# Retention followed by a gated FFN: the 64x64 matmuls of a block in stretches of three, three and two items instead of four pairs

## The chip, the cores and the metric

One NeuronCore of a Trainium2 chip runs the whole program in one launch. The metric is the device time in microseconds (us) of one execution; the time before is the median of three runs, 890.47 us (888.77 to 890.8). The engines are called as in the profile: PE is TensorE's matmuls and PEld its weight loads, DVE is VectorE, ACT is ScalarE, POOL is GpSimd, SP is the engine that issues most DMAs.

## The reference, cut to what matters

```python
# q, k, v: (8 batches, 8 heads, 576 positions, 64)
scores = q @ k^T / 8                          # per batch and head
ret    = (scores * gamma[h] ** (i - j) where i >= j, else 0) @ v
x      = ret, laid out as (8 * 576 tokens, 512)
h      = x @ w_in                             # 512 -> 2048
out    = (h - tanh(h)) @ w_out                # 2048 -> 512
```

The retention can be computed position block by position block. With a block of 64 positions, the output of a block is q times a running state (the sum of k^T v over all earlier blocks) plus the block's own masked scores times v. The powers of gamma are put into q and v by tables, so that one 0/1 mask serves every block.

## The kernel before

**Blocks and items.** The 576 positions are nine blocks of 64 (numbered 0 to 8, `n` for the FFN, `c0` for the retention). A block has eight items, one per batch (`b`); item number `j` is 8 times the block plus `b`. The eight heads of an item lie as two halves of 64 partitions times four. The FFN of a block takes all 8 x 64 = 512 tokens at once.

**The two kinds of PE work.** The FFN is made of `mm1(n, f)` (L320, twelve 128x512 matmuls in words of fp32r: hidden slice `f` of 16) and `mm2(n, f)` (L379, twelve more, accumulated over all `f` in the four banks `o0` to `o3`). `activate` (L345) turns the result of `mm1` into the words `gh` and `gl`: tanh on ACT (L353), a subtraction on DVE (L354), a cast on ACT (L355), a subtraction on DVE (L356). The retention is made of 64x64 fp32 matmuls, all issued in `run` (L247, line L252 in the profile): `m_score` (8 calls per item), `m_state` (8), `m_out` (16). A call appears as two matmuls in the profile. `run` takes two lists and issues two calls of the one and two of the other in turn; scores and states use the two array quadrants on the diagonal, outputs use the other two, so that the two lists run side by side.

**An entry.** `entry(p, sc)` (L289) does, in one stretch of PE work, for the pair of items `2p`, `2p+1`: their outputs and state updates, and the scores of the next pair. Then DVE masks those scores into `pm` (L263, needed by the outputs of the next entry), ACT casts the outputs to `xh` (L278), DVE makes `xl` (L280) and adds the new state (L311). After that the next-but-one pair is loaded (1 MB, L171, on SP's queue) and scaled on POOL (`prep`, L185 and L186). `pm`, `new` and `own` have one buffer each, the PSUM tag `h` has two banks, which `mm1` and the scores `sc` share.

**The order of the work** is written out by hand, and `in_order` (L47) keeps every engine's instructions in the order in which they are written. The parts around the change are:

- L529 to L568 (`seq`): `mm1` of blocks 0 and 1, whose results are spilled, while the weights are converted to words by `step()` (a third of a weight tile per call: DVE L105, L110, L112, L124 and ACT L95, L98, L117); the entries of block 1 lie in it.
- L570 to L583 (`late`, 32 steps `k`): each step issues the two words of step `k+1` (`words`, ACT L375, DVE L376), the tanh and the subtraction of step `k+2` (`resume`, ACT L368, DVE L369), fetches a spilled tile, calls `step()` (twice while `k < 4`), and then issues `mm2`. Entries of block 2 stand ahead of `mm2` at `k` = 3, 8, 13 and 18.
- L585 to L596: for blocks `n` = 2 to 8, `mm1(n, f)` and the `mm2` of one slice earlier in turn; the four entries of block `n+1` stand between them at `f` = 1, 5, 9 and 13.

Of the kernel before, what the change touches and what calls it, by code (L numbers as in the profile page):

```python
# [9 lines left out]
F32 = mybir.dt.float32  # L10
# [9 lines left out]
P = 128  # L20
NF = DF // P
# [9 lines left out]
STEP = float(np.arctanh(0.5) / (1.06 * 2.0**-15))  # L31
WARM = 26

NP = NC * B // 2


class Parts:
# [30 lines left out]
def retention_ffn(ctx: ExitStack, tc: tile.TileContext, ins, out, spill):  # L68
# [81 lines left out]
            step()  # L150


    loaded, scored, xs, qtabs = {}, {}, {}, {}

    def load_qtab(c):
        if c not in qtabs:
# [6 lines left out]
    def load_pair(p, u=None):  # L163

        if p >= NP:
            return
        c, pr = divmod(p, B // 2)
        load_qtab(c)
        a = loaded["pair", p] if u == 1 else pool.tile([P, 2, 4, 4, C], F32, tag="a", name=f"a{p}")
        if u is None:  # L170
            nc.sync.dma_start(a, qkv_d[c - 1, 2 * pr : 2 * pr + 2].rearrange("u p t i s -> p u t i s"))  # L171
        else:
            nc.sync.dma_start(a[:, u], qkv_d[c - 1, 2 * pr + u])
        loaded[2 * p], loaded[2 * p + 1] = a[:, 0], a[:, 1]
        loaded["pair", p] = a
        loaded["qv", p] = a[:, :, 0], a[:, :, 2]

    def prep(p, q=True):
        if p >= NP:
            return  # L180
        c = p // (B // 2)
        a = loaded["pair", p]
        if q:
            table = qtabs[c].unsqueeze(1).broadcast_to([P, 2, 4, C])
            nc.gpsimd.tensor_tensor(a[:, :, 0], a[:, :, 0], table, op=ALU.mult)  # L185
        nc.gpsimd.tensor_tensor(  # L186
            a[:, :, 2], a[:, :, 2], vtab[:, c].unsqueeze(1).unsqueeze(3).broadcast_to([P, 2, 4, D]), op=ALU.mult
        )

    def load_early(p):
        c, pr = divmod(p, B // 2)
        if pr < 2:
            return load_pair(p)
        src = qkv_d[c - 1, 2 * pr : 2 * pr + 2].rearrange("u p t i s -> p u t i s")
        parts = []
        for t in range(2):
            parts.append(const.tile([P, 2, 2, 4, C], F32, tag=f"wo{2 * (pr - 2) + t}", name=f"a_early{p}_{t}"))
            nc.sync.dma_start(parts[t], src[:, :, 2 * t : 2 * t + 2])  # L200
            behind(tc, pace[-1])
        for u in range(2):
            loaded[2 * p + u] = Parts([part[:, u] for part in parts])
        loaded["qv", p] = parts[0][:, :, 0], parts[1][:, :, 0]

    def scale_q(p):
        q, table = loaded["qv", p][0], qtabs[p // (B // 2)]
        nc.vector.tensor_tensor(q, q, table.unsqueeze(1).broadcast_to([P, 2, 4, C]), op=ALU.mult)

    def scale_v(p):  # L210
        v = loaded["qv", p][1]
# [43 lines left out]
    def after_score(j, sc, n):  # L255

        if j < B:

            pm = pool.tile([P, 2, 4, C], F32, tag="gh", name=f"pm{j}")
            nc.vector.tensor_tensor(pm[:, 0], sc[:, 0], decay, op=ALU.mult)  # L260
        else:
            pm = pool.tile([P, 2, 4, C], F32, tag="pm", bufs=1, name=f"pm{j}")
            nc.vector.tensor_tensor(  # L263
                pm[:, :n].rearrange("p u i q -> p (u i) q"), sc.rearrange("p u i q -> p (u i) q"),
                mask.unsqueeze(1).broadcast_to([P, 4 * n, C]), op=ALU.mult,
            )
        for u in range(n):
            scored[j + u] = pm[:, u]
# [20 lines left out]
    def entry(p, sc, more=None):  # L289
        c0, pr = divmod(p, B // 2)  # L290
        new = psp.tile([P, 2, 4, D], F32, tag="new", bufs=1, name=f"new{p}")
        o = psp.tile([P, 2, 4, C], F32, tag="own", bufs=1, name=f"own{p}")
        same, other = [], []
        for u in range(2):
            if p + 1 < NP:
                same += m_score(2 * p + 2 + u, sc[:, u])
            other += m_out(2 * p + u, o[:, u])
        if c0 < NC - 1:
            for u in range(2):
                same += m_state(2 * p + u, new[:, u])  # L300
        if more is not None:
            same += more[0]
        run(same, other)
        if p + 1 < NP:
            after_score(2 * p + 2, sc, 2)
        after_out(2 * p, o, 2)
        if more is not None:
            more[1]()
        if c0 < NC - 1:
            st = state[:, 2 * pr : 2 * pr + 2]  # L310
            nc.vector.tensor_tensor(st, new, st, op=ALU.add)  # L311
        if p >= B:
            load_pair(p + 2)
            prep(p + 2)


    gs, ops, homes, obs = {}, {}, {}, {}
# [27 lines left out]
    def activate(n, f, h, g):  # L345
        if n == NC - 1 and f == NF - 1:

            both = pool.tile([P, 2, BLK], F32R, tag="a", name="both")
# [6 lines left out]
        nc.scalar.copy(gh, g)  # L355
        nc.vector.tensor_tensor(gl, g, gh.bitcast(F32), op=ALU.subtract)  # L356
        gs[n, f] = (gh, gl)
# [127 lines left out]
    for j in range(B):  # L485
        o = psp.tile([P, 8, C], F32, tag=("o2", "o3", "own")[j % 3], bufs=1, name=f"own_first{j}")[:, :4]
        run(score_first(j + 2) if j < B - 2 else [], m_out(j, o))
        if j < B - 2:
            after_score(j + 2, firsts[j + 2].unsqueeze(1), 1)
            paced(lambda: load_paced(7) if j == 0 else upto("load", j + 2) if j < 4 else None)  # L490
        if j == 3:
            nc.sync.dma_start(vtab, vtab_d)
            nc.sync.dma_start(krows[0], krows_d[0])
            load_early(B // 2)
            nc.sync.dma_start(mask, mask_d)
            upto("load", 7)
            load_early(B // 2 + 1)
        if j < 4:
            busy(*((2, BLK) if j < 2 else (1, BLK // 2)))
        low = after_out(j, o.unsqueeze(1), 1, j < 6)  # L500
        if j == 0:
            paced(lambda: upto("load", 2))
        if j >= 6:
            lows.append(low)
        if j < 4:
            step()
        if j == 5:
            guard(*stream[1], True)
        if j == 6:
            upto("guard", 2)  # L510
# [15 lines left out]
    late = [(1, f) for f in turn] + [(0, f) for f in range(NF)]  # L526
    early = {5: 4, 8: 5, 10: 6, 14: 7}
    scales = {2: 4, 4: 5, 7: 6, 9: 7, 13: 8}
    for k, (n, f) in enumerate(seq):  # L529
        last_two = k - (len(seq) - 2)  # L530
        if k in (2, 7):
            scale_k(k // 4)
        if k + 1 in early:
            scale_v(early[k + 1])
        if last_two < 0:
            step()
        else:
# [4 lines left out]
            if k < 24:  # L542
                step()
        if k in scales:
            scale_q(scales[k])
        upto("load", k + (7 if k < 11 else 6))
        if k in (2, 5):
            load_early(B // 2 + 2 + (k - 2) // 3)
        if k in (9, 10):
            load_pair(B, k - 9)  # L550
        for f in [f for f in home if home[f] == (7, 13, 12, 11, 10)[k - NF]] if NF <= k < NF + 5 else []:
            nc.sync.dma_start(spill[0, f], homes[home[f]][:, (f + 1) % 2 if f > 1 else f])
        if k == 3:
            nc.sync.dma_start(krows[1], krows_d[1])
            behind(tc, pace[-1])
            sc = scores_of(B // 2 - 1)
            ms, done = first_states(0, "new")
            run(m_score(B, sc[:, 0]) + m_score(B + 1, sc[:, 1]) + ms, [])
            after_score(B, sc, 2)
            done()  # L560
        if k in early:
            p = early[k]
            more = first_states(2 * (p - 3), f"o{(p + 1) % 2}") if p < B - 1 else None
            entry(p, scores_of(p), more)
        if k == 14:
            load_pair(B + 1)
        if k in (26, 28):
            prep(B + (k - 26) // 2, k == 28)  # L568
    p = B
    for k, (n, f) in enumerate(late):  # L570
        if 0 < k < len(late) - 1:
            words(*late[k + 1])
# [3 lines left out]
            fetch(*late[k + 4])  # L576
        for _ in range(2 if k < 4 else 1):
            step()
        if k in (3, 8, 13, 18):
            entry(p, psp.tile([P, 2, 4, C], F32, tag="h", bufs=2, name=f"s{n}_{f}"))  # L580
            p += 1
        if k < len(late) - 1:
            mm2(n, f)  # L583

# [69 lines left out]
```

## Time and profile before

| | |
|---|---|
| median of the runs | 890.47 us (888.77, 890.47, 890.8) |
| profiled execution | 891.8 us |
| span in it, first to last instruction | 890.0 us |
| PE matmuls, busy | 877.6 us |
| DVE, ACT, POOL busy | 363.3, 287.7, 67.7 us |
| mean granted TensorE clock | 0.995 |
| 64x64 stretches for blocks 2 to 8 | 28 |

Busy time of PE is the union of its matmuls from start to modelled end; matmuls overlap, so PE reads as busy even where a handover between two kinds of matmul costs time. Such costs are read from the start times of consecutive matmuls. A row of a timeline merges instructions of the same kind that follow each other; its first number is the start, its second the length of the merged piece.

### The profile page before, as it was taken

The page shows a single profiled execution, that of the slowest core. Times are in us where ns is not written, and L with a number is a line of the kernel's source. Part 1 is how long each engine was busy: PE and PEld are TensorE (multiplying, and loading weights), DVE is VectorE, ACT ScalarE, POOL GpSimd, SP SyncE. Part 2 cuts the span into 40 slices and gives each one's busy share as a digit, 9 for nine tenths or more (in the row PEclk, how much of TensorE's full clock was granted, in tenths as well). Part 3 has the DMA queues.
Part 4 walks back from the last instruction along what each step waited for, and adds up shares of the span by engine and source line. Part 5 has one row for each costly group of instructions (what it writes and reads, how often), then busy time and mean ns, then how long its engine had stood idle before and what let it go on. Part 6 is the DMA issues. An engine that isn't in the chain of part 4 may idle for free.

```text
span 890.0 us, 17595 instructions
## 1 busy us (share of the span) xinstructions
PE 877.6 (99%) x7848; PEld 724.3 (81%) x7848; DVE 363.3 (41%) x548; ACT 287.7 (32%) x503; POOL 67.7 (8%) x59
## 2 busy tenths in 40 slices
PE   7999999999999999999999999999999999999997
PEld 6777878788888888888888888888888888888886
DVE  6879777653432332333233233323323322222222
ACT  4887774443222222222222222222222221222222
POOL 0001001210111110111111111111000111000000
PEclk8999999999999999999999999999999999999999
DMA  9966965551311131102111131113111201002001
GB/s 354 325 231 212 342 193 171 167 167 48 96 54 49 48 96 49 54 30 68 47 54 49 49 95 54 49 48 96 49 54 47 62 35 48 1 1 49 1 1 47
DMA packets 31372, 82.06 MB, mean 92 GB/s; under 512 B 3776, under 2 KB 4928, under 8 KB 31296
## 3 DMA queue, kind: packets, MB, share of 16 engines
q1 hardware_dynamic: 30768, 80.02, 27.8%
q8 instruction: 61, 1.00, 0.5%
q10 hardware_dynamic: 528, 0.92, 0.3%
q14 instruction: 15, 0.12, 0.0%
HBM read 63.62 MB, written 17.30 MB: 91 GB/s over the span
## 4 chain that ended last, share of the span: by engine, by line
PE 90%; DMA 3%; DVE 3%; ACT 2%; issue 0%; SPq 0%; DVEq 0%
PE o L393 44%; PE h L327 38%; PE s L252 3%; DMA rwo<-in_w_out_dram 2%; PE new L252 2%; PE own L252 2%; DMA rwi<-in_w_in_dram 1%; DVE mo L110 0%; DVE mo L112 0%; ACT mi L95 0%; ACT mi L98 0%; PE new_first L252 0%; DVE mi L105 0%; DVE wi L124 0%; ACT wi L117 0%
## 5 line engine op out<-in xcount | busy, mean ns | idle before, releaser
L327 PE MATMUL h<-xh,wi 128*128 128x512 f32 x1152 | 307.0, 392 | 2.7 <-ACT g L339 0.8
L393 PE MATMUL o<-wo,gh 128*128 128x512 f32 x1144 | 291.6, 393 | 0.4 <-DVE ob L412 0.4
L327 PEld LDWEIGHTS h<-xh,wi 128*128 128x128 f32 x1152 | 216.3, 189 | 49.7 <-ACT g L339 1.3
L393 PEld LDWEIGHTS o<-wo,gh 128*128 128x128 f32 x1144 | 212.3, 188 | 46.8 <-DVE ob L412 1.5
L354 DVE TENSOR_TENSOR g<-h,g 128x512 f32<-128x512 f32 x114 | 78.8, 691 | 367.1 <-ACT g L353 367.1
L353 ACT ACTIVATE g<-h 128x512 f32<-128x512 f32 x114 | 68.3, 599 | 420.9 <-PE h L327 420.1
L393 PE MATMUL o<-wo,gl 128*128 128x512 f32 x572 | 157.3, 389 | 0.0
L327 PE MATMUL h<-xl,wi 128*128 128x512 f32 x576 | 154.5, 390 | 0.0
L327 PEld LDWEIGHTS h<-xl,wi 128*128 128x128 f32 x576 | 108.7, 189 | 22.9
L393 PEld LDWEIGHTS o<-wo,gl 128*128 128x128 f32 x572 | 107.4, 188 | 22.3
L356 DVE TENSOR_TENSOR gl<-g,gh 128x512 fp32r<-128x512 f32 x113 | 81.0, 717 | 77.5 <-ACT gh L355 70.0
L355 ACT CAST gh<-g 128x512 fp32r<-128x512 f32 x113 | 70.1, 620 | 86.2 <-DVE g L354 86.2
L185 POOL TENSOR_TENSOR a<-a,qtab 128x512 f32<-128x512 f32 x27 | 36.3, 1344 | 605.7 <-DMA a<-in_qkv_dram 547.3
L252 PE MATMUL own<-a,state 64*64 64x64 f32 x960 | 58.9, 221 | 0.0
L252 PE MATMUL own<-pm,a 64*64 64x64 f32 x960 | 57.5, 218 | 0.0
L252 PEld LDWEIGHTS own<-a,state 64*64 64x64 f32 x960 | 47.8, 134 | 0.4 <-issue 0.4
L252 PEld LDWEIGHTS own<-pm,a 64*64 64x64 f32 x960 | 48.0, 135 | 0.0
L252 PEld LDWEIGHTS s<-a 64*64 64x64 f32 x960 | 30.3, 134 | 10.6 <-issue 10.2
L186 POOL TENSOR_TENSOR a<-a,vtab 128x512 f32<-128x512 f32 x28 | 32.2, 1152 | 67.4 <-DVE mi L112 67.4
L252 PE MATMUL s<-a 64*64 64x64 f32 x960 | 34.4, 221 | 0.0
L376 DVE TENSOR_TENSOR gl<-s,gh 128x512 fp32r<-128x512 f32 x30 | 21.6, 720 | 31.2 <-PE o L393 24.4
L375 ACT CAST gh<-s 128x512 fp32r<-128x512 f32 x30 | 18.6, 621 | 39.0 <-PE o L393 27.4
(67 smaller groups left out, 465.0 us busy)
## 6 DMA issues: line engine op xcount, KB each, us to landing
a<-in_qkv_dram SPq DMA_DIRECT2D x29, 1024.0 KB, 5.2
out_dram<-ob SPq DMA_DIRECT2D x69, 128.0 KB, 2.4
rwi<-in_w_in_dram SPq DMA_DIRECT2D x16, 512.0 KB, 5.8
rwo<-in_w_out_dram SPq DMA_DIRECT2D x16, 512.0 KB, 5.1
s<-spill_dram SPq DMA_DIRECT2D x30, 256.0 KB, 2.7
spill_dram<-g SPq DMA_DIRECT2D x20, 256.0 KB, 5.2
a<-in_first_dram SPq DMA_DIRECT2D x7, 384.0 KB, 5.0
spill_dram<-home SPq DMA_DIRECT2D x10, 256.0 KB, 6.3
```

What stands on the lines that cost most here:

```text
L185: nc.gpsimd.tensor_tensor(a[:, :, 0], a[:, :, 0], table, op=ALU.mult)
L186: nc.gpsimd.tensor_tensor(a[:, :, 2], a[:, :, 2], vtab[:, c].unsqueeze(1).unsqueeze(3).broadcast_to([P, 2, 4, D]), op=ALU.mult)
L252: nc.tensor.matmul(out_, w, x, start=start, stop=stop)
L327: nc.tensor.matmul(hp, win[f][:, a, cc, :], x[:, cc, :], start=(k == 0), stop=(k == 3 * NCC - 1))
L353: nc.scalar.activation(g, h, AF.Tanh)
L354: nc.vector.tensor_tensor(g, h, g, op=ALU.subtract)
L355: nc.scalar.copy(gh, g)
L356: nc.vector.tensor_tensor(gl, g, gh.bitcast(F32), op=ALU.subtract)
L375: nc.scalar.copy(gh, g)
L376: nc.vector.tensor_tensor(gl, g, gh.bitcast(F32), op=ALU.subtract)
L393: nc.tensor.matmul(ops[n][t], g[:, t * P : (t + 1) * P], wout[f_][:, a, :], start=(f_ == first and k == 0), stop=(f_ == final and k == 2),)
```

## The change

Pairs become parts: the q/k half and the v/k half of a pair of items are separate tiles (`qk` with two buffers, `vr` with one), and a single item has a tile `one`, in place of the two buffers `a`. `pm` has no buffer any more and is written over the k columns of its own item once the scores are done. From block 2 on, `entry3(j)` stands for a stretch: at `b` = 0 and 3 it takes three items (outputs and states of `j`, `j+1`, `j+2`), at `b` = 6 two. With three, it runs in three parts: the scores of item `j+2` with half of the outputs of `j`; the states of `j` and `j+1` and half of the scores of the following pair with the rest of the outputs; the other half of the scores and the state of `j+2` with the outputs of `j+2`. All scores and new states take banks of the tag `h` by turns; `own` and `new` hold the outputs of the pair and of the single item. In `late` the stretches stand at `k` = 3, 9 and 15; for `n` = 2 to 7 at `f` = 1, 9 and 13, each now behind the `mm2` of one slice earlier and followed at once by the `mm2` of its own slice.

```diff
@@ after_score
-            pm = pool.tile([P, 2, 4, C], F32, tag="pm", bufs=1, name=f"pm{j}")
+            pm = parts[j, 0][:, :, 1]
             nc.vector.tensor_tensor(
...
+    def bank(name, tag):
+        return psp.tile([P, 2, 4, D], F32, tag=tag, bufs=2 if tag == "h" else 1, name=name)
+
+    def add_state(j, new, n=2):
+        st = state[:, j % B : j % B + n]
+        nc.vector.tensor_tensor(st, new, st, op=ALU.add)
+
+    def pair(what, j, bank):
+        return what(j, bank[:, 0]) + what(j + 1, bank[:, 1])
...
+    def entry3(j):
+        c0, b = divmod(j, B)
+        single, states = b + 2 < B, c0 < NC - 1
+        then = j + 2 + single
+        o = bank(f"own{j}", "own")
+        outs = pair(m_out, j, o)
+        if single:
+            sc = bank(f"s{j + 2}", "h")
+            run(m_score(j + 2, sc[:, 0]), outs[:8])
+            outs = outs[8:]
+            after_score(j + 2, sc[:, :1], 1)
+        same, scores = [], []
+        if states:
+            new = bank(f"new{j}", "h")
+            same += pair(m_state, j, new)
+        if then < NI:
+            sc = bank(f"s{then}", "h")
+            scores = pair(m_score, then, sc)
+        n = 8 if single else 16
+        run(same + scores[:n], outs)
+        if states:
+            add_state(j, new)
+        low = after_out(j, o, 2, False)
+        if single:
+            o, same = bank(f"own{j + 2}", "new"), scores[n:]
+            if states:
+                new = bank(f"new{j + 2}", "h")
+                same += m_state(j + 2, new[:, 0])
+            run(same, m_out(j + 2, o[:, 0]))
+        low()
+        if then < NI:
+            after_score(then, sc, 2)
+        if single:
+            low = after_out(j + 2, o[:, :1], 1, False)
+            if states:
+                add_state(j + 2, new[:, :1], 1)
+            low()
+
+        after = then + 2 + ((then + 2) % B != 0)
+        if then < NI:
+            load_part(then, 1)
+            prep(then, 1)
+            if then % B + 2 < B:
+                load_one(then + 2)
+                prep(then + 2, 1, 1)
+                prep(then + 2, 0, 1)
+            load_part(after, 0)
+            prep(after, 0)
...
@@ late
-        if k in (3, 8, 13, 18):
-            entry(p, psp.tile([P, 2, 4, C], F32, tag="h", bufs=2, name=f"s{n}_{f}"))
-            p += 1
+        if k in (3, 9, 15):
+            entry3(first + 3 * (3, 9, 15).index(k))
         if k < len(late) - 1:
             mm2(n, f)
...
     for n in range(2, NC):
         for f in range(NF):
             mm1(n, f)
-            if n + 1 < NC and f % 4 == 1:
-
-                sc = psp.tile([P, 2, 4, C], F32, tag="h", bufs=2, name=f"s{n}_{f}")
-                entry((n + 1) * B // 2 + f // 4, sc)
             todo.append((n, f))
-            if (n, f) != (NC - 1, NF - 2):
+            if len(todo) > 1 and (n, f) != (NC - 1, NF - 2):
+                mm2(*todo.pop(0))
+            if n + 1 < NC and f in (1, 9, 13):
+
+                entry3((n + 1) * B + 3 * (1, 9, 13).index(f))
                 mm2(*todo.pop(0))
```

`load_part(j, t)` loads one half of a pair (512 KB), `load_one(j)` a single item (512 KB), and `prep(j, t, n)` scales one of the two halves on POOL. In `seq` the same bytes as before are loaded at the same steps, in parts. The entries of block 1 stay pairs.

More of the change, by code (lines that the diff above doesn't have):

```diff
@@ L32 @@
 WARM = 26
-NP = NC * B // 2
+NI = NC * B
 class Parts:
@@ L150, in units @@
             step()
-    loaded, scored, xs, qtabs = {}, {}, {}, {}
+    loaded, scored, xs, qtabs, parts = {}, {}, {}, {}, {}
     def load_qtab(c):
@@ L161, in load_qtab, with load_part @@
             nc.sync.dma_start(qtabs[c], qtab_d[c - 1])
-    def load_pair(p, u=None):
-        if p >= NP:
+    def load_part(j, t):
+        if j >= NI:
             return
[L167 to L171, printed above, removed]
-        else:
[L173 to L176, printed above, removed]
@@ L178, in prep @@
-    def prep(p, q=True):
-        if p >= NP:
-            return
[L181 to L204, printed above, removed]
@@ L206, in scale_q @@
-    def scale_q(p):
-        q, table = loaded["qv", p][0], qtabs[p // (B // 2)]
+        c, b = divmod(j, B)
+        if t == 0:
+            load_qtab(c)
+        early = c == 1 and b // 2
+        if early and early > 1:
+            part = const.tile([P, 2, 2, 4, C], F32, tag=f"wo{2 * (early - 2) + t}", name=f"early{j}_{t}")
+        elif early and t == 1:
+            part = pool.tile([P, 2, 2, 4, C], F32, tag="one", bufs=1, name=f"vr{j}")
+        else:
+            part = pool.tile([P, 2, 2, 4, C], F32, tag=("qk", "vr")[t], bufs=2 - t, name=f"{('qk', 'vr')[t]}{j}")
@@ new lines, in load_part, with load_pair, load_one @@
+        nc.sync.dma_start(part, qkv_d[c - 1, b : b + 2, :, 2 * t : 2 * t + 2].rearrange("u p t i s -> p u t i s"))
+        if early and early > 1:
+            behind(tc, pace[-1])
+        parts[j, t] = part
+        for u in range(2):
+            loaded.setdefault(j + u, Parts([None, None])).parts[t] = part[:, u]
+    def load_pair(j):
+        for t in range(2):
+            load_part(j, t)
+    def load_one(j):
+        c, b = divmod(j, B)
+        a = pool.tile([P, 4, 4, C], F32, tag="one", bufs=1, name=f"one{j}")
+        nc.sync.dma_start(a, qkv_d[c - 1, b])
+        loaded[j] = Parts([a[:, 0:2], a[:, 2:4]])
+        parts[j, 0], parts[j, 1] = a[:, 0:2].unsqueeze(1), a[:, 2:4].unsqueeze(1)
@@ L208, in scale_q, with prep, scale_v @@
+    def prep(j, t, n=2):
+        if j >= NI:
+            return
+        c = j // B
+        a = parts[j, t][:, :, 0]
+        if t == 0:
+            table = qtabs[c].unsqueeze(1).broadcast_to([P, n, 4, C])
+        else:
+            table = vtab[:, c].unsqueeze(1).unsqueeze(3).broadcast_to([P, n, 4, D])
+        nc.gpsimd.tensor_tensor(a, a, table, op=ALU.mult)
+    def scale_q(j):
+        q, table = parts[j, 0][:, :, 0], qtabs[j // B]
         nc.vector.tensor_tensor(q, q, table.unsqueeze(1).broadcast_to([P, 2, 4, C]), op=ALU.mult)
-    def scale_v(p):
-        v = loaded["qv", p][1]
+    def scale_v(j):
+        v = parts[j, 1][:, :, 0]
@@ L261, in after_score @@
         else:
-            pm = pool.tile([P, 2, 4, C], F32, tag="pm", bufs=1, name=f"pm{j}")
+            pm = parts[j, 0][:, :, 1]
             nc.vector.tensor_tensor(
-                pm[:, :n].rearrange("p u i q -> p (u i) q"), sc.rearrange("p u i q -> p (u i) q"),
-                mask.unsqueeze(1).broadcast_to([P, 4 * n, C]), op=ALU.mult,
+                pm, sc, mask.unsqueeze(1).unsqueeze(1).broadcast_to([P, n, 4, C]), op=ALU.mult,
             )
@@ L287, in first_states, with entry @@
         return ms, lambda: nc.scalar.copy(state[:, b : b + 2], new)
[L289 to L300, printed above, removed]
+    def bank(name, tag):
[5 more added lines that the diff above has]
+        return what(j, bank[:, 0]) + what(j + 1, bank[:, 1])
+    def entry(j, sc, more=None):
+        new, o = bank(f"new{j}", "new"), bank(f"own{j}", "own")
+        same, other = pair(m_score, j + 2, sc) + pair(m_state, j, new), pair(m_out, j, o)
         if more is not None:
@@ L303, in entry @@
         run(same, other)
-        if p + 1 < NP:
-            after_score(2 * p + 2, sc, 2)
-        after_out(2 * p, o, 2)
+        after_score(j + 2, sc, 2)
+        after_out(j, o, 2)
         if more is not None:
             more[1]()
[L309 to L314, printed above, removed]
+        add_state(j, new)
[20 more added lines that the diff above has]
+        if states:
+            add_state(j, new)
+        low = after_out(j, o, 2, False)
[23 more added lines that the diff above has]
+            prep(after, 0)
     gs, ops, homes, obs = {}, {}, {}, {}
@@ L346, in activate @@
         if n == NC - 1 and f == NF - 1:
-            both = pool.tile([P, 2, BLK], F32R, tag="a", name="both")
+            both = pool.tile([P, 2, BLK], F32R, tag="qk", name="both")
             gh, gl = both[:, 0], both[:, 1]
@@ L493, in retention_ffn @@
             nc.sync.dma_start(krows[0], krows_d[0])
-            load_early(B // 2)
+            load_pair(B)
             nc.sync.dma_start(mask, mask_d)
             upto("load", 7)
-            load_early(B // 2 + 1)
+            load_pair(B + 2)
         if j < 4:
@@ L528, in retention_ffn @@
     scales = {2: 4, 4: 5, 7: 6, 9: 7, 13: 8}
+    first = 2 * B
     for k, (n, f) in enumerate(seq):
@@ L533, in retention_ffn @@
         if k + 1 in early:
-            scale_v(early[k + 1])
+            scale_v(2 * early[k + 1])
         if last_two < 0:
@@ L544, in retention_ffn @@
         if k in scales:
-            scale_q(scales[k])
+            scale_q(2 * scales[k])
         upto("load", k + (7 if k < 11 else 6))
         if k in (2, 5):
-            load_early(B // 2 + 2 + (k - 2) // 3)
+            load_pair(B + 4 + 2 * (k - 2) // 3)
         if k in (9, 10):
-            load_pair(B, k - 9)
+            load_part(first, k - 9)
         for f in [f for f in home if home[f] == (7, 13, 12, 11, 10)[k - NF]] if NF <= k < NF + 5 else []:
@@ L555, in retention_ffn @@
             behind(tc, pace[-1])
-            sc = scores_of(B // 2 - 1)
+            sc = scores_of(3)
             ms, done = first_states(0, "new")
-            run(m_score(B, sc[:, 0]) + m_score(B + 1, sc[:, 1]) + ms, [])
+            run(pair(m_score, B, sc) + ms, [])
             after_score(B, sc, 2)
@@ L563, in retention_ffn @@
             more = first_states(2 * (p - 3), f"o{(p + 1) % 2}") if p < B - 1 else None
-            entry(p, scores_of(p), more)
+            entry(2 * p, scores_of(p), more)
         if k == 14:
[L566 to L569, printed above, removed]
+            load_one(first + 2)
+            load_part(first + 3, 0)
+        if k == 26:
+            prep(first, 1)
+        if k == 28:
+            prep(first + 2, 1, 1)
+            prep(first + 2, 0, 1)
+            prep(first + 3, 0)
     for k, (n, f) in enumerate(late):
```

## The prediction

> **What bounds the kernel now.** I read the page first: the span, the engines, the clock.
>
> ```profile
> span 890.0 us, 17595 instructions
> ...
> PE 877.6 (99%) x7848; PEld 724.3 (81%) x7848; DVE 363.3 (41%) x548; ACT 287.7 (32%) x503; POOL 67.7 (8%) x59
> ...
> PEclk8999999999999999999999999999999999999999
> ```
>
> PE is busy nearly throughout at full clock and nothing else is busy half of the time, so only what changes the spacing of matmuls on PE changes the end. Next, the chain of waits around one entry of a late block, which is PE from end to end.
>
> ```profile
> 253.09 2.95 PE o L393 x12
> ...
> 272.36 2.72 PE h L327 x12
> 275.08 0.20 PE s L252 x2
> ...
> 277.11 2.95 PE o L393 x12
> ```
>
> A dense group of twelve takes 2.72 us. The first group after an entry takes 2.95. From one such group to the next (253.09 to 277.11) pass 24.02 us, of which seven more groups take 7 x 2.72 = 19.04; the entry costs 24.02 - 8 x 2.72 = 2.26 us. The timeline of PE shows how much of that is matmuls:
>
> ```profile
> 250.68 0.39 PE L327 MATMUL h<-xh,wi 128*128 128x512 f32 x1
> ...
> 251.11 0.23 PE L252 MATMUL s<-a 64*64 64x64 f32 x2
> ...
> 252.86 0.23 PE L252 MATMUL new<-a 64*64 64x64 f32 x2
> ```
>
> Four matmuls, one per quadrant, start together. Between the rows at 251.11 and 252.86 lie 30 such steps: 1.75 / 30 = 58.3 ns each. A pair has 128 matmuls, 32 steps, 1.87 us. The other 2.26 - 1.87 = 0.39 us is the price of going from 128x512 to 64x64 matmuls and back, whatever stands between. The waits of PEld show its first half, thirty times, with no engine as its cause:
>
> ```profile
> PEld s L252 <- issue: 10.6, 30, 0.4
> ```
>
> **The gain.** Blocks 2 to 8 go from four stretches to three: 7 x 0.39 = 2.7 us removed. The steps stay: three items take 8 + 24 + 16 = 48 steps, so a block has 48 + 48 + 32 = 128, as four pairs had.
>
> **The waits that it adds.** An old entry reads nothing made inside it. A stretch of three does, twice. At step 24 the scores of the following pair go into the bank from which DVE must first have masked item `j+2` (and step 32 reads that `pm`). At step 40 the state of `j+2` goes into the bank that `add_state` of the pair must first have read. PE issues in order, so behind either wait stands everything: the rest of the stretch, its `mm2`, and through them ACT's `xh` and DVE's `xl`. DVE works in order too, so the question is what DVE has in front of that mask. Without a stall, step 24 starts 24 x 58.3 ns = 1.40 us after the stretch.
>
> At `k` = 3 the mask is far down the queue. The old pair entry stands at the same place with the same DVE work ahead of it. DVE:
>
> ```profile
> 133.22 0.68 DVE L376 TENSOR_TENSOR gl<-s,gh 128x512 fp32r<-128x512 f32 x1
> 133.82 0.69 DVE L369 TENSOR_TENSOR s<-s,th 128x512 f32<-128x512 f32 x1
> 134.42 0.69 DVE L110 SCALAR_TENSOR_TENSOR mo<-rwo,mo 128x512 int32<-128x512 int32 x1
> 135.14 0.69 DVE L112 SCALAR_TENSOR_TENSOR mo<-rwo,mo 128x512 int32<-128x512 int32 x1
> 137.04 0.69 DVE L376 TENSOR_TENSOR gl<-s,gh 128x512 fp32r<-128x512 f32 x1 [1.21 <-ACT gh L375]
> 137.65 0.69 DVE L369 TENSOR_TENSOR s<-s,th 128x512 f32<-128x512 f32 x1
> 138.25 0.69 DVE L124 TENSOR_TENSOR wo<-mo,wo 128x512 fp32r<-128x512 f32 x1
> 138.86 0.69 DVE L263 TENSOR_TENSOR pm<-s,mask 128x512 f32<-128x512 f32 x1
> ```
>
> ACT, which holds up the `gl` at 137.04, and PE's entry and the `mm2` behind it:
>
> ```profile
> 135.87 0.62 ACT L117 CAST wo<-mo 128x512 fp32r<-128x512 f32 x1 [2.24 <-DVE mo L112]
> 136.40 0.61 ACT L375 CAST gh<-s 128x512 fp32r<-128x512 f32 x1
> ```
>
> ```profile
> 133.01 0.27 PE L252 MATMUL s<-a 64*64 64x64 f32 x2
> ...
> 135.03 2.11 PE L393 MATMUL o<-wo,gh 128*128 128x512 f32 x8
> ```
>
> The entry starts at 133.01, and its mask starts only at 138.86, back to back behind the last weight conversion (L110, L112, ACT's cast, L124) and the words and subtraction of the next steps. Nothing in this chain waits for PE work behind the entry: the `gl` at 137.04 waits for ACT's cast, and that for DVE. Before, this lag costs nothing, since the mask is needed only at the next entry. Now PE needs it at 133.01 + 1.40 = 134.41. The prices of the two DVE operations:
>
> ```profile
> L311 DVE TENSOR_TENSOR state<-new,state 128x512 f32<-128x512 f32 x28 | 19.1, 682 | 0.0
> ...
> L260 DVE TENSOR_TENSOR pm<-s_first,decay 128x256 f32<-128x256 f32 x8 | 3.4, 423 | 6.5 <-PE s_first L252 6.0 <-PE own_first L252 0.3
> ```
>
> The mask of one item is half the size: 0.42 us (L260 has that shape), done at 139.28. PE stands still for 139.3 - 134.4 = 4.9 us. Nothing gives that back, as PE is the bound afterwards too. The `mm2` at this step then starts late, and DVE, which had no slack here (`gl` ends at 137.73, the group of eight plus four after 135.03 ends its starts near 137.8), gains some.
>
> At `k` = 9 DVE has no conversions left. The nearest row is the entry at `k` = 13:
>
> ```profile
> 164.71 0.27 PE L252 MATMUL s<-a 64*64 64x64 f32 x2
> ```
>
> ```profile
> 165.50 0.68 DVE L369 TENSOR_TENSOR s<-s,th 128x512 f32<-128x512 f32 x1
> ```
>
> DVE is free at 166.18, 1.47 us after the start; with 0.42 the mask is done at 1.9, against 1.40: 0.5 us. Bounds: 0 (the subtraction starts earlier) and 1.3 (two more operations ahead of it).
>
> In blocks 3 to 7 (two stretches of three each, ten in all) the new place, behind an `mm2`, gives DVE time:
>
> ```profile
> 253.11 0.69 DVE L356 TENSOR_TENSOR gl<-g,gh 128x512 fp32r<-128x512 f32 x1 [0.68 <-ACT gh L355]
> ```
>
> `gl` ends 253.80 - 250.68 = 3.1 us after the last matmul of its `mm1` starts; the `mm2` that now stands between takes 2.72, and the switch some 0.3, so DVE is free about when the stretch starts. The mask of item `j+2` then runs from 0.75 to 1.2: in time for 1.40. `add_state` is tighter: the pair's last state matmul starts at step 23 (1.39 us with the slow first step), lasts 0.22, then 0.68 on DVE and two handovers of some 0.05 (estimates from adjacent rows): done at 2.40. PE wants to load the weights of step 40 at about 2.33. That is 0.07 us ten times, 0.7 us; bounds 0 and 2. Block 8 has no states, and at `b` = 6 nothing made in the stretch is read in it: no wait.
>
> **The rest, at nothing.** POOL scales in four operations instead of two after a stretch; the page has it 8% busy, and the parts are used a stretch later, 16 us or more. SP issues three loads of 512 KB instead of one of 1 MB after a stretch, each waiting for PE to free its part; queued behind them are spill fetches, asked for four steps (11 us) ahead, and output stores. If that cover is gone, one fetch late by a load, under 3 us, hits `late` alone. The masks written over the k columns wait for the scores that they already wait for. DVE has two more, smaller, operations per stretch of three.
>
> **The clock.** PE has no standstill of 4.9 us before. The nearest is at the start:
>
> ```profile
> 13.05 0.27 PE L252 MATMUL s_first<-a 64*64 64x64 f32 x2 [1.44 <-DMA a<-in_first_dram]
> ```
>
> ```profile
> 14.79:21.61 6.82, 6.23 (x41) 5.07 (x38) 6.27 (x12) 3.89 (x8) 0.00 (x0) 0.50 1.02 396
> ```
>
> After 1.44 us of idle PE among thin 64x64 work the granted clock is 0.50 from 14.79 to 21.61, 6.82 us. A longer standstill in the middle of 64x64 work should do the same. In part of that time PE stands still anyway; I take two thirds of it, 4.6 us, as work at half speed, 2.3 us lost; bounds 0 (not triggered) and 3.4 (half of 6.82). [...]
>
> **The sum.** -2.7 + 4.9 + 0.5 + 0.7 + 2.3 = +5.7 us. The profiled execution took 891.8 (span 890.0 and 1.8 around it), so its like takes 897.5; the median of the runs is 1.3 below it, 890.47, and from there I forecast 896.1.
>
> **Rivals.** A difference of 0.2% is 1.8 us, about what a measurement of this kernel can tell.
>
> 1. The clock is not halved, the rest holds: 890.47 + 3.4 = 893.9. [...] Against it: the start needed only 1.44 us. Chance 0.2.
> 2. Faster: the mask at `k` = 3 is early enough, and only the removed switches count: -2.7 + 0.5 + 0.7 = -1.5, 889.0. It decides at 134.4: DVE would have to be 4.9 us ahead of where it was. The conversions ahead of it (three DVE operations at 0.6 and 1.2 us of waiting for ACT) are 3 us, so even their absence isn't enough. Chance 0.07.
> 3. The stall at `k` = 3 is about half as long and the clock holds: about 0 to +1.7, 891.3. Chance 0.06.
> 4. The instructions don't come fast enough, and each of the 14 stretches of three stalls for a fetch. The DMA queues show the fetches:
>
> ```profile
> q8 instruction: 61, 1.00, 0.5%
> ```
>
> 61 packets for 2 x 7848 PE instructions are one per 257; 0.5% of 16 engines' 890 us is 1.2 us per packet. A pair has 256 instructions and passes one boundary; its 1.87 us cover one fetch. A stretch of three has 384, one boundary or two by its place; with two, the second fetch has 1.87 us. At worst 14 x 1.2 = 17 us; with half of it on top of the forecast, 904.6. [...] Chance 0.05.
>
> The forecast has what is left, 0.62.
>
> **The numbers.** Low: case 1 with the waits at their lower bounds, 890.47 - 2.7 + 4.9 = 892.7, so 892.5. High: all upper bounds, -2.7 + 4.9 + 1.3 + 2 + 3.4 = +8.9, 899.4, so 899. Outside lie cases 2 to 4, 0.18. Faster 0.07 (case 2), same 0.07 (case 3 and a little of case 1), slower 0.86.
>
> **What would show it.** In the profile after: DVE's `pm` of a single item near 138.9 at `k` = 3, PE idle for some 5 us in that stretch, released by it; a clock below 1 in the slices after it; half a microsecond of such a wait at `k` = 9; stretches of blocks 3 to 8 about 3.2 us long (0.39 + 48 x 58.3 ns) with a short wait for `state` near the end; 21 switches instead of 28. I am wrong if PE runs through the stretch at `k` = 3 without a gap, or if the later stretches show gaps that no DVE operation ends.

## The result, and the profile after

The change costs 14.1 us: 903.78 us median (902.31 to 904.1, four runs) against 889.67 us (888.77 to 890.8, four runs), a ratio of 1.0157 with a 95% interval of 1.0144 to 1.017. The forecast was 896.1 us, with a range up to 899. The direction was right and the size was not. The profiled execution took 904.1 us. Its page (span, engines, clock, chain, and the group of the first weight loads of `mm2`, which is L442 now):

```profile
span 902.3 us, 17730 instructions
PE 880.5 (98%) x7848; PEld 725.6 (80%) x7848; DVE 371.3 (41%) x568; ACT 289.4 (32%) x510; POOL 69.6 (8%) x73
PEclk9999999999999999999999999999999999999999
PE 83%; DVE 6%; DMA 4%; ACT 4%; issue 2%; SPq 0%; DVEq 0%; ACTq 0%
L442 PEld LDWEIGHTS o<-wo,gh 128*128 128x128 f32 x1144 | 212.5, 188 | 52.4 <-DVE ob L461 5.3
```

PE's busy time grew by only 2.9 us (877.6 to 880.5), so most of the loss is PE standing still. From the first 64x64 matmul of block 2 to the last matmul of the program pass 752.07 us before (133.01 to 885.07) and 766.16 us after (131.36 to 897.52): the loss lies there. (The earlier part, which the change hardly touches, ended 1.65 us sooner in this execution; there the clock was at half for 3.41 us, and for 6.82 us in the execution before. So it is in part chance that the two medians differ by the same 14.1 us.) Three places come first.

**The stretch at `k` = 3.** PE and DVE:

```profile
131.36 0.27 PE L255 MATMUL s<-one 64*64 64x64 f32 x2
...
132.76 0.22 PE L255 MATMUL own<-qk,vr 64*64 64x64 f32 x2
137.73 0.27 PE L255 MATMUL s<-qk 64*64 64x64 f32 x2 [4.74 <-issue]
```

```profile
136.01 0.68 DVE L418 TENSOR_TENSOR s<-s,th 128x512 f32<-128x512 f32 x1
136.61 0.68 DVE L124 TENSOR_TENSOR wo<-mo,wo 128x512 fp32r<-128x512 f32 x1
137.21 0.42 DVE L267 TENSOR_TENSOR one<-s,mask 128x256 f32<-128x256 f32 x1
```

Step 24 should have started at 132.82. It starts at 137.73, 0.1 us after the mask of the single item ends at 137.63. The mask runs straight behind the last weight conversion (L124). The page puts PE's wait down to "issue"; the times of the two rows name its cause. The clock then halves:

```profile
138.00:141.30 3.30, 3.30 (x97) 3.06 (x87) 2.62 (x5) 0.96 (x2) 0.00 (x0) 0.50 0.45 147
```

**The ten stretches of three in blocks 3 to 7.** The first of them on PE, then on DVE:

```profile
236.99 0.27 PE L255 MATMUL s<-one 64*64 64x64 f32 x2
...
238.74 0.23 PE L255 MATMUL own<-qk,state 64*64 64x64 f32 x2
...
239.32 0.23 PE L255 MATMUL own<-one 64*64 64x64 f32 x2
239.78 0.27 PE L255 MATMUL new<-one 64*64 64x64 f32 x2 [0.23 <-DVE state L297]
```

```profile
239.03 0.69 DVE L297 TENSOR_TENSOR state<-new,state 128x512 f32<-128x512 f32 x1 [0.82 <-PE own L255]
```

At step 40 PE waits 0.45 us in place of a step of 0.06. The `add_state` that it waits for does not start when the pair's new states are there. It starts at 239.03, when the output matmul of 238.74 has ended (238.97): that one reads the old `state`, which `add_state` overwrites. From the matmul ahead of such a stretch to the one behind it pass 3.74 us, against 3.28 us in the two stretches of block 8, which have as many steps and no states: 0.46 us each.

**The block ends.** `mm2(3, 0)` on PE, its weight loads and DVE (three of its four banks, then the fourth):

```profile
330.76 0.84 PE L442 MATMUL o<-wo,gh 128*128 128x512 f32 x3
...
331.14 0.69 DVE L461 COPY ob<-o 128x512 f32<-128x512 f32 x1 [2.33 <-PE h L376]
...
331.89 0.77 PEld L442 LDWEIGHTS o<-wo,gh 128*128 128x128 f32 x4 [0.71 <-DVE ob L461]
331.89 0.98 PE L442 MATMUL o<-wo,gh 128*128 128x512 f32 x3 [0.29 <-DVE ob L461]
```

The weight load for the fourth bank waits until DVE has copied out what the block before left there, into `ob`. Such a gap stands in `mm2(n, 0)` for `n` = 2 to 7, 0.36 to 0.45 us, and the matmuls behind it take 0.14 to 0.17 more: 3.4 us in all. The kernel before has such a gap of 0.33 us in `mm2(8, 0)`, the only one of these that has no entry ahead of it:

```profile
803.20 0.84 PE L393 MATMUL o<-wo,gh 128*128 128x512 f32 x3
804.21 0.98 PE L393 MATMUL o<-wo,gh 128*128 128x512 f32 x3 [0.16 <-DVE ob L412]
```

In the views of waits, before and after stand so (total, times, longest):

```profile
PEld o L393 <- DVE ob L412: 1.5, 3, 0.6
```

```profile
PEld o L442 <- DVE ob L461: 5.3, 8, 0.7
```

A fourth place is a single one. At 193.8 PE waits 1.4 us longer than usual, for the words of a spilled tile whose fetch came late. SP's queue and ACT:

```profile
184.49 4.83 SPq L463 DMA_DIRECT2D out_dram<-ob  x4
189.41 1.50 SPq L412 DMA_DIRECT2D s<-spill_dram  x3
```

```profile
193.31 0.63 ACT L417 ACTIVATE th<-s 128x512 f32<-128x512 f32 x1 [4.58 <-DMA s<-spill_dram]
```

The fetches stand behind the issues of the stores, and three of these issues wait for the three loads of the stretch at `k` = 15 to land. SP's waits from 180 to 192 us (total, times, longest):

```profile
SPq L463 <- DMA one<-in_qkv_dram: 1.4, 1, 1.4
SPq L463 <- DMA qk<-in_qkv_dram: 0.8, 1, 0.8
SPq L463 <- DMA vr<-in_qkv_dram: 0.6, 1, 0.6
```

**The account**, from the start times of consecutive matmuls, the slower ones right behind a switch or a gap included:

| term | forecast, us | trace after, us |
|---|---|---|
| seven switches fewer | -2.7 | -2.7 |
| standstill at `k` = 3 | +4.9 | +4.9 |
| half clock after it | +2.3 | +1.6 |
| waits at `k` = 9 | +0.5 | +1.0 |
| `add_state`, ten stretches | +0.7 | +4.6 |
| first `mm2` of blocks 2 to 7 | 0 | +3.4 |
| late fetch at 193.8 | 0 | +1.6 |
| other | 0 | -0.3 |
| sum | +5.7 | +14.1 |

### The profile page after: what moved, and what is told of

Same layout as the page of the kernel before. It is cut to its first block, busy times and chain, and to the rows that moved or that the text cites. A ratio compares the mean times of both kernels' runs of the same rounds, so it can differ in the third digit from the quotient of the medians.

```text
span 902.3 us, 17730 instructions
## 1 busy us (share of the span) xinstructions
PE 880.5 (98%) x7848; PEld 725.6 (80%) x7848; DVE 371.3 (41%) x568; ACT 289.4 (32%) x510; POOL 69.6 (8%) x73
## 4 chain that ended last, share of the span: by engine, by line
PE 83%; DVE 6%; DMA 4%; ACT 4%; issue 2%; SPq 0%; DVEq 0%; ACTq 0%
PE o L442 41%; PE h L376 35%; PE new L255 3%; PE s L255 2%; PE own L255 2%; DMA rwo<-in_w_out_dram 1%; DMA out_dram<-ob 1%; DVE state L297 1%; DMA a<-in_first_dram 1%; DVE ob L461 1%; DVE mo L110 1%; ACT ob L459 1%; DVE g L403 1%; DVE wo L124 1%; ACT g L402 0%
## 5 line engine op out<-in xcount | busy, mean ns | idle before, releaser
L376 PE MATMUL h<-xh,wi 128*128 128x512 f32 x1152 | 302.1, 390 | 1.3 <-issue 0.5
L442 PE MATMUL o<-wo,gh 128*128 128x512 f32 x1144 | 293.0, 393 | 3.3 <-DVE ob L461 1.8
L442 PEld LDWEIGHTS o<-wo,gh 128*128 128x128 f32 x1144 | 212.5, 188 | 52.4 <-DVE ob L461 5.3
L442 PE MATMUL o<-wo,gl 128*128 128x512 f32 x572 | 157.4, 389 | 0.0
L442 PEld LDWEIGHTS o<-wo,gl 128*128 128x128 f32 x572 | 107.4, 188 | 22.5
L405 DVE TENSOR_TENSOR gl<-g,gh 128x512 fp32r<-128x512 f32 x113 | 83.6, 740 | 77.6 <-ACT gh L404 72.8
L206 POOL TENSOR_TENSOR vr<-vr,vtab 128x512 f32<-128x512 f32 x21 | 22.2, 1058 | 672.0 <-DMA vr<-in_qkv_dram 588.1
L255 PE MATMUL own<-qk,state 64*64 64x64 f32 x736 | 45.6, 222 | 0.0
L255 PE MATMUL own<-qk,vr 64*64 64x64 f32 x736 | 44.5, 219 | 0.0
L281 ACT CAST xh<-own 128x512 fp32r<-128x512 f32 (+1 forms) x39 | 19.9, 510 | 71.1 <-PE own L255 71.1
L255 PEld LDWEIGHTS own<-qk,state 64*64 64x64 f32 x736 | 36.8, 135 | 0.4 <-issue 0.4
L255 PEld LDWEIGHTS own<-qk,vr 64*64 64x64 f32 x736 | 37.0, 136 | 0.0
L255 PE MATMUL s<-qk 64*64 64x64 f32 x736 | 26.6, 222 | 5.0 <-issue 5.0
L255 PEld LDWEIGHTS s<-qk 64*64 64x64 f32 x736 | 24.2, 138 | 6.3 <-issue 5.6
```

The source lines that it names most:

```text
L206: nc.gpsimd.tensor_tensor(a, a, table, op=ALU.mult)
L255: nc.tensor.matmul(out_, w, x, start=start, stop=stop)
L281: nc.scalar.copy(xh, o)
L376: nc.tensor.matmul(hp, win[f][:, a, cc, :], x[:, cc, :], start=(k == 0), stop=(k == 3 * NCC - 1))
L442: nc.tensor.matmul(ops[n][t], g[:, t * P : (t + 1) * P], wout[f_][:, a, :], start=(f_ == first and k == 0), stop=(f_ == final and k == 2),)
```

## The experiments

My theory after the result: the standstill of DVE's queue is as forecast, and three costs were missed, the wait on readers of `state`, the new place of the first `mm2`, and the late fetch. The main rivals were that the stretches themselves are slowed by instruction fetches, and that the loads of 1.5 MB behind a stretch cause the gaps at the block ends. All times below stand beside the kernel before on the same chip, 889.21 us for the first four kernels and 889.44 us for the last four.

### Two tiles for the state, by turns

```diff
+    other = const.tile([P, 2, 4, D], F32, name="other")
+    def state_of(c0, b):
+        return other[:, b // 4] if b in (1, 4) and c0 % 2 == 0 else state[:, b]
...
+        if n == 2 and b in (0, 3, 4):
+            for u in range(2):
+                nc.vector.tensor_tensor(state_of(c0 + 1, b + u), new[:, u], state_of(c0, b + u), op=ALU.add)
```

The later item of the pair writes its new state into another tile than the one its outputs still read.

> The changed kernel, but items 1 and 4 of a block keep their state in two tiles by turns, so that adding the new state of a pair in a stretch of three writes no state that the outputs of that stretch still read (the addition becomes two of one item each). Theory: the 0.45 us gap at step 40 is there because the addition has to wait for the last output matmul that reads the old state, near step 30, not for the state matmuls, which are done at step 24. Then the gap falls from 449 ns to under 0.15 us in the ten stretches of blocks 3 to 7 and the kernel becomes some 3 to 4 us faster than the changed kernel, 900 to 901. Rival: the gap is the time of the addition behind the state matmuls and the hand-over of the bank; then it stays at 0.45 us or grows, since there are two additions, and the time stays at 903 to 905.

It took 901.99 us (900.3 to 904.94), a spread that overlaps with that of the changed kernel, so the trace has to decide. DVE and PE in the same stretch as above, which starts at 238.78 here:

```profile
240.44 0.42 DVE L303 TENSOR_TENSOR state<-new,state 128x256 f32<-128x256 f32 x1 [0.44 <-PE new L259]
240.78 0.41 DVE L303 TENSOR_TENSOR other<-new,state 128x256 f32<-128x256 f32 x1
```

```profile
241.12 0.23 PE L259 MATMUL own<-one 64*64 64x64 f32 x2
241.34 0.27 PE L259 MATMUL new<-one 64*64 64x64 f32 x2
```

DVE's wait is for `new` now, no longer for `own`, and the gap is 0.22 us in place of 0.45, in all ten stretches; at `k` = 9 it is gone. What remains is the two additions, which begin only when all the state matmuls of the pair are done. I had expected more than half of the wait to go. The additions end 2.41 us after the stretch's start (241.19), in place of 2.73, so the reading of `state` did hold them up; but step 40 begins 0.15 us behind them here, and 0.06 us behind the addition in the changed kernel, and no run shows why. From the first stretch of block 3 to the last matmul pass 658.8 us in the trace, against 660.5 after; the half clock behind `k` = 3 lasted longer here (below), which hides part of the gain in the total.

### A buffer of its own for the fourth `ob`

```diff
-            ob = pool.tile([P, DM], F32, tag="cv", bufs=3, name=f"ob{n}_{t}")
+            ob = pool.tile([P, DM], F32, tag="g" if t == 3 else "cv", bufs=3, name=f"ob{n}_{t}")
```

> The changed kernel, but the fourth output tile of a block (t = 3) takes a buffer of the tag g instead of the tag cv. Theory: the gap of about 0.67 us ahead of the first mm2 of blocks 3 to 8 is there because the copy of the fourth output waits for the store of the first to land (three buffers), and the new order puts that mm2 one mm1 behind the last mm2 of the block before, with no stretch between. Then the six gaps vanish and the kernel becomes 3 to 3.5 us faster than the changed one, 900.3 to 900.8. Rival: the copies are late because DVE is busy with the words of mm1; then the gaps stay and the time stays within 1 us of 903.8.

It took 900.19 us (898.98 to 900.9), 3.6 us less than the changed kernel. All six gaps are gone; the view of waits has this left:

```profile
PEld o L442 <- DVE ob L461: 0.5, 1, 0.5
```

The fourth copy had waited for the store of the first one to free its buffer: in the block shown above that store landed at 330.92, and the copy started at 331.14. With a buffer ready, it follows the second copy without a gap and is early enough.

### The old kernel's pairs, with the new order of `mm2`

```diff
             mm1(n, f)
+            todo.append((n, f))
+            if len(todo) > 1 and (n, f) != (NC - 1, NF - 2):
+                mm2(*todo.pop(0))
             if n + 1 < NC and f % 4 == 1:
                 entry((n + 1) * B // 2 + f // 4, sc)
-            todo.append((n, f))
-            if (n, f) != (NC - 1, NF - 2):
                 mm2(*todo.pop(0))
```

> The kernel before, with its four pairs a block, but with the order of the second matmul that the changed kernel has: `mm2` of the item before goes ahead of each entry at f = 1, 5, 9, 13, and the next `mm2` right behind the stretch. Theory (the gaps of about 0.5 us ahead of the first `mm2` of blocks 3 to 8 come from this order, because `mm2(n, 0)` now follows `mm2(n-1, 15)` with one first matmul between and no stretch, and so comes before `ob` has a free buffer): six to seven gaps of 0.4 to 0.6 us at the block ends, 2.5 to 3.3 us in all, time 891.7 to 892.7. Rival (the gaps come from the stretches of three, which store more at the wrong moment): no such gaps, time within 0.5 us of the kernel before, 889.2.

It took 892.16 us (891.57 to 894.36), ratio 1.003 (1.0018 to 1.0042): 2.7 us more than before, without any stretch of three.

```profile
PEld o L393 <- DVE ob L412: 5.0, 8, 0.8
```

The waits are those of the changed kernel (5.3 us, 8 times). The order alone makes them. In the kernel before, the entry at `f` = 1 stood ahead of `mm2(n, 0)`, and its 2.26 us covered the store; now `mm2(n, 0)` comes first. (The expectation numbers these blocks one too high: they are `n` = 2 to 7.)

### Block 2's stretches later

```diff
-        if k in (3, 9, 15):
-            entry3(first + 3 * (3, 9, 15).index(k))
+        if k in (8, 13, 18):
+            entry3(first + 3 * (8, 13, 18).index(k))
```

> The changed kernel, but the three stretches of block 2 stand at k = 8, 13 and 18 in place of 3, 9 and 15. Theory: the standstill of 4.9 us and the half clock behind it come from DVE's and ACT's conversions that end only at k = 3; at k = 8 the mask is late by 0.5 to 1.3 us and at k = 13 by 0.5, and the clock stays at 1. The late spill fetch (1.5 us at 193.8) goes too, as the loads no longer stand ahead of the stores of block 1. Sum: 4.9 + 1.4 + 1.5 less 0.5 to 1, some 7 us faster than the changed kernel, 896 to 898. Rival: a stretch of three in this phase stalls wherever it stands, since the words and subtractions of every step stand ahead of its mask; then the standstill shrinks only to 2 to 3 us and the time stays above 899.

It took 898.56 us (898.19 to 899.52), 5.2 us less than the changed kernel. The standstill, the half clock and the late fetch are gone, 8.1 us by the account. Some of it comes back. Where no entry stands at `k` = 3 any more, nothing covers the conversions:

```profile
132.55 0.69 DVE L112 SCALAR_TENSOR_TENSOR mo<-rwo,mo 128x512 int32<-128x512 int32 x1
133.28 0.62 ACT L117 CAST wo<-mo 128x512 fp32r<-128x512 f32 x1 [2.24 <-DVE mo L112]
133.80 0.61 ACT L424 CAST gh<-s 128x512 fp32r<-128x512 f32 x1
...
134.47 0.50 PE L442 MATMUL o<-wo,gh 128*128 128x512 f32 x1 [0.89 <-ACT gh L424]
```

PE starts this `mm2` 1.06 us late. The stretches at `k` = 8 and 13 have both waits (0.50 and 0.44 us) and in addition a gap of 0.47 and 0.35 us near the end, among matmuls into banks already in use. These are the only stretches of 384 instructions in this kernel that by my count contain two boundaries of 256 instructions. The length is my estimate from the pages before and after: 61 instruction packets for 15,696 weight loads and matmuls of PE, one per 257.

### Block 2's stretches one step later

```diff
-        if k in (3, 9, 15):
-            entry3(first + 3 * (3, 9, 15).index(k))
+        if k in (4, 10, 16):
+            entry3(first + 3 * (4, 10, 16).index(k))
```

> The changed kernel with block 2's stretches at k = 4, 10, 16 in place of 3, 9, 15; by the count of instructions each still holds one boundary. VectorE's lead grows by an entry's work less a first matmul of 3.3 us, so the standstill at the first stretch should be 3.2 to 4.0 us in place of 4.96. [...] The late fetch at 193.8 may go or stay with the loads of the last stretch (1.5 us more).

It took 902.75 us (901.32 to 903.82). PE, DVE's mask, and the clock after the standstill:

```profile
135.95 0.22 PE L255 MATMUL own<-qk,vr 64*64 64x64 f32 x2
139.22 0.27 PE L255 MATMUL s<-qk 64*64 64x64 f32 x2 [3.04 <-issue]
```

```profile
138.70 0.42 DVE L267 TENSOR_TENSOR one<-s,mask 128x256 f32<-128x256 f32 x1
```

```profile
140.00:143.00 3.00, 2.94 (x62) 2.44 (x53) 2.59 (x5) 0.93 (x2) 0.00 (x0) 0.51 0.62 202
```

PE goes on 0.1 us behind the mask again. The standstill is 3.26 us long, in the expected range, and the clock halves all the same: after 3.04 us of idle PE it is 0.51 from 140 to 143. In the changed kernel PE was idle for 4.74 us before its half clock.

### Two boundaries in a stretch, and a control

```diff
-            if n + 1 < NC and f in (1, 9, 13):
+            if n + 1 < NC and f in (4, 9, 13):
```

> The changed kernel, but the first stretch of a block stands at f = 4 in place of 1, which by the count of PE instructions (48 per f, 144 for three) puts two boundaries of 256 instructions into it instead of one; the stretches at 9 and 13 keep their places and their count. [...] Rival: the second boundary comes before its instructions have arrived; then gaps of 0.3 to 1.2 us appear in the six moved stretches that no engine's work ends, and the kernel is 2 to 7 us slower, 906 to 911.

It took 908.38 us (906.64 to 909.85), 4.6 us more than the changed kernel. In the trace 3.1 us of this lie in four stretches; block 2 also starts 1.7 us later in it. Of the moved stretches four stand still for 0.93, 0.94, 1.28 and 1.48 us, one has 0.38 us at step 40, and the one of block 8 has no gap. The third of them:

```profile
452.21 0.22 PE L255 MATMUL s<-qk 64*64 64x64 f32 x1
453.49 0.27 PE L255 MATMUL s<-qk 64*64 64x64 f32 x2 [1.06 <-issue]
```

PE stops before step 40, in the middle of scores that go into a bank already in use. The stretches at `f` = 9, which stay where they were, keep their 0.45 us. I had expected the moved stretches to stay 3.27 us long and the time to stay within 0.7 us of 903.8, which failed: stops like those of rival 4 of the prediction came up, in a kernel that is not the change. The control moves the same stretch only to `f` = 2, where the count gives one boundary:

```diff
-            if n + 1 < NC and f in (1, 9, 13):
+            if n + 1 < NC and f in (2, 9, 13):
```

> A control for the run with two boundaries: the first stretch of blocks 3 to 7 moves from f = 1 to f = 2, where by the count it still holds one boundary of 256 instructions. Theory (the stalls of 0.9 to 1.5 us in the run with f = 4 come from the second boundary): no gap beside the known 0.45 us at step 40, time 903.0 to 904.6 as for the changed kernel. Rival (moving the stretch away from f = 1 as such brings the gaps, by loads or by VectorE): gaps of about 1 us in the moved stretches, 906 to 909.

It took 903.89 us (903.76 to 905.92), as the changed kernel does. In the stretch of the same block:

```profile
440.51 0.22 PE L255 MATMUL own<-one 64*64 64x64 f32 x2
440.97 0.27 PE L255 MATMUL new<-one 64*64 64x64 f32 x2 [0.23 <-DVE state L297]
```

There is only the known wait in this stretch and in the other moved ones of blocks 3 to 7. One stop of 0.3 us that the trace puts down to no engine stands 1 us behind the moved stretch of block 7, in `mm2` (636.82). So moving a stretch as such does not make the stops of about 1 us; moving it to a place with two boundaries does.

### All found costs taken away

```diff
-            ob = pool.tile([P, DM], F32, tag="cv", bufs=3, name=f"ob{n}_{t}")
+            ob = pool.tile([P, DM], F32, tag="g" if t == 3 else "cv", bufs=3, name=f"ob{n}_{t}")
...
-        single, states = b + 2 < B, c0 < NC - 1
+        single, states = c0 > 2 and b + 2 < B, c0 < NC - 1
...
-        if k in (3, 9, 15):
-            entry3(first + 3 * (3, 9, 15).index(k))
+        if k in (3, 8, 13, 18):
+            entry3(first + 2 * (3, 8, 13, 18).index(k))
```

Beside these it has the two tiles for the state, and block 2's loads go by pairs.

> The changed kernel with all its found costs taken away: block 2 keeps its four pairs at k = 3, 8, 13, 18 as before, the stretches of three come from block 3 on, items 1 and 4 keep their state in two tiles by turns, and the fourth copy of `ob` has a buffer of its own. Theory (the three costs found are all there is): no standstill and no half clock, no gap at the block ends, gaps of about 0.22 us (0.16 over a step) at step 40 in ten stretches; six switches fewer at 0.36 to 0.39 us are 2.2 to 2.3 us gained, 1.6 us of it given back, so 888.0 to 889.5, as before or 0.1 per cent faster. Rival (something else in the stretches of three costs time, such as loads of 1.5 MB that hold up stores and fetches): over 891.

It took 889.92 us (887.84 to 892.59), ratio 0.9999 (0.9986 to 1.0011): the 14.1 us are gone, and the kernel is as fast as before. Its first stretch of three:

```profile
231.86 0.22 PE L259 MATMUL own<-one 64*64 64x64 f32 x2
232.09 0.27 PE L259 MATMUL new<-one 64*64 64x64 f32 x2
```

Each of the ten stretches takes 3.51 us in place of 3.28, so 10 x 0.23 = 2.3 us are lost there. A block with one stretch fewer and two such waits takes 96.12 us here and 96.05 before, so a switch is worth 0.46 - 0.07 = 0.39 us, and six give 2.3 us. That is why nothing is won in total. No version here is faster than the kernel before.

## Why the prediction was wrong

**The step that failed: "`add_state` is tighter: the pair's last state matmul starts at step 23 ... 0.07 us ten times".** The term of the sum was mis-sized: 0.7 us stood there, its upper bound was 2, and it measured 4.6. I let `add_state` start when its input `new` was complete. It also overwrites `state`, and the outputs of the pair read `state` up to 238.97, that is 1.98 us after the stretch's start and not 1.61. With this 0.37 us more, my own sum gives a wait of 0.44 us, close to what is seen. The run with two tiles shows it: DVE's releaser changes from `own` to `new`, the additions are done at 2.41 us, where the sum had 2.40, and the wait is halved. That half of it stays, though the sum left 0.07, is open: step 40 begins 0.15 us behind the additions there.

**The second step that failed: "The rest, at nothing".** I costed loads, POOL and SP there, and did not cost the new place of `mm2` at all, though the diff moves it. Between the last `mm2` of one block and the first of the next only one `mm1` is left, without the entry's 2.26 us, and the wait for the fourth `ob` costs 3.4 us. The profile before had it already in `mm2(8, 0)`. The run with pairs in the new order has these waits alone, and the run with another buffer has none.

**The late fetch** was named in the same part with a bound of under 3 us and left at nothing; it costs 1.6 us here. It is gone in the runs with other stretches in block 2. With block 2 as in the change its size varies: 1.1 us in the run with the `ob` buffer, 0.5 with `f` = 2, none with two tiles and with `f` = 4. That the loads of the stretch at `k` = 15 delay the stores ahead of the fetches on SP's queue is read from the view of SP's waits, and no run tested it alone.

**Right:** the standstill at `k` = 3 (4.9 forecast, 4.96 from start to start, of which one step is 0.06), with its cause in DVE's queue; the price of a switch (0.39 us); that the clock halves, of which I had taken 2.3 us, and 1.6 came, because it lasted 3.41 us (0.50 from 137.97 to 141.38) and not 6.82. The half clock at the program's start, by which the prediction went, varies itself: it lasted 6.82 us before and 3.41 in the changed kernel, and, judged by their mean clocks (0.995, 1.0 and 0.997), there is none in the runs with the `ob` buffer, with `k` = 8, 13, 18 and with `k` = 4, 10, 16. The wait at `k` = 9 was forecast at 0.5 for the mask, which is right (0.44 us over a step); the second wait there, for `add_state`, is the missed reader again. Rival 1, the clock that is not halved, is refuted by that same 0.50; rivals 2 and 3 by the standstill.

**Rival 4** doesn't occur at the places of the change: no stretch of the kernel after has a gap that the waits do not explain. At other places there are stops that no wait explains, 0.93 to 1.48 us long in the run with `f` = 4; that a late fetch makes them is not shown.

## What to carry to other kernels

An operation that updates a buffer in place is late by its last reader as well as by its last input (here 1.98 us after the stretch's start and not 1.61), so for every wait in a merged stretch both have to be looked up. When a change moves a step, cost the step at its new place with all that it waits for, stores of its old buffers included; what stood ahead of it may have been the cover. Merging saves a switch each time, here 0.39 us, and a single wait of that size inside the merged stretch takes it back.

## What the runs showed of the hardware

- A stretch of 384 64x64 instructions with two boundaries of 256 in it has a stop of 0.35 to 1.48 us in six of seven cases (`f` = 4 and the stretches at `k` = 8 and 13); with one, none was seen inside a stretch. Counted in the trace (PE's weight loads, matmuls and semaphore waits in order), all six stops, and the one behind a stretch of the run with `f` = 2, begin at the same place modulo 256, 192 or 193, which agrees with the length estimated from the packets, one per 257. What stops PE there isn't settled: in the case shown one instruction packet runs in the window and ends 0.1 us before PE stops, and none runs during the stop.
- The half clock lasted 3.4 us after standstills of 4.96 us (the changed kernel) and 3.26 us, but 6.8 us in the runs with two tiles, the `ob` buffer, `f` = 4 and `f` = 2, whose standstills are within 0.02 us as long as the one after. In these four it began 1.0 to 2.4 us before PE went on, in the other two 0.2 and 0.8 us after. In the `ob` run:

```profile
135.00:141.70 6.70, 4.37 (x100) 4.00 (x101) 4.88 (x9) 1.45 (x3) 0.00 (x0) 0.50 0.39 123
```
